# Identity products in TensorE's gaps, means in two column halves, a mask pattern made once, and a new order of work

## The chip, the cores and the metric

The kernel runs on one core of a Trainium2 chip. The metric is the device time of one execution in microseconds (us). A core has TensorE (PE, matrix products; loading of their stationary operand is shown as PEld), VectorE (DVE), ScalarE (ACT), GpSimd (POOL) and SyncE (SP, which issues all loads and stores here). Each engine works off its own list of instructions in order and waits on semaphores for the others.

## The reference

Sparse attention over 4 batches of 8 heads, 768 positions and 64 columns, followed by a two-branch layer:

```python
k_sum = k.reshape(B, H, nb, block, D).max(axis=3)      # block = 32, nb = 24
v_sum = v.reshape(B, H, nb, block, D).mean(axis=3)
scores_l = scale * q @ k.T      # kept where |i - j| < 16, else -1e9
scores_s = scale * q @ k_sum.T + log(32)
a = softmax(concat(scores_l, scores_s))
x = (a @ concat(v, v_sum))      # then heads side by side: 3072 x 512
out = maximum(x @ w1, x @ w2) @ w_out      # 512 -> 1024 -> 512
```

So each query sees at most 31 neighbours and all 24 block summaries.

## The kernel before

A helper records every operation as a task with its engine or engines, an estimated time, its inputs and outputs and a priority (`op`, line 107; `copy`, line 278, whose instructions all carry line 271 of `move`). Then `Plan.run` (line 132) walks through the tasks with these estimates, gives each engine the ready task of lowest priority number and buffers from rings, and so writes out one fixed order for each engine. The constants `C` (line 23) are priorities, the order of the loads (`first` for batch 0, `later` for the others) and which engines may do which copy. `caps` limits how many of the eight PSUM banks each kind of result may hold. On the chip nothing of the plan is left but the order and the semaphores.

Attention is done by batch and by pair of heads (`hp`, 0 to 3):

- `load_kq` (329) and `load_v` (337) load 384 KB of k or q of a pair, or 768 KB of v of four heads.
- `prep` (382): k and q are cast to bf16 (`kqb`), turned by six transposes each (line 393), and placed as `kx` and `qx`. For each of 12 tiles of 64 queries, `kx` holds 96 local keys and 24 block maxima (line 406), so that one product gives all 120 scores of a query.
- `place_v` (343): v is cast into `vx`, shifted copies are made for the odd tiles, and the block means are made by six products of 128 rows with `amean`, 256 columns wide (line 361), copied into `vx` and spread to all tiles.
- `scores` (425): 12 or 14 products for six tiles, each on 64 rows of the array (line 442). Two heads use the two halves of its rows. For batch 0 the mask is added by TensorE, with an identity times the pattern `hide` (434); for the others `pb` is multiplied by `mask` after the exponential (449, 454).
- `values` (462): 12 products on 64 columns of the array each (471), a reciprocal and a multiplication give x (482, 484); x of two pairs is turned by six transposes (494) and copied to `xt`.

The layer is rewritten: max(xw1, xw2) = xw1 + relu(x(w2 - w1)). `make_w12` (518) makes `wd` = w2 - w1 in four quarters and turns w1 (531); `make_w1o` (546) makes w1 @ w_out once (552, 32 products). `maxout` (560) then has, for each half batch of 384 rows (`grp`), 8 blocks of hidden columns of 4 products (567) with a relu each (572 on ACT, 574 on DVE), and three output tiles of 4 products with `w1o` (584) and 8 with `wo` (591), copied to `o` and stored.

TensorE has three ways of working here: the whole array, half its rows (scores) and half its columns (values). The planner counts 0.08 us (`TURN`) for a change between them, and when it has the choice it prefers a task in the mode that it is in:

```python
if e == "PE" and mode:
    able.sort(key=lambda t: t.mode != mode)
t = next((t for t in able if self.slots(t, now)), None)
```

`fixed_parts` (287) makes the constants: `hide` by wide memsets and selects on POOL (305 to 310), `amean` (313) and `mask` (323), also on POOL.

Of the kernel before, what the change touches and what calls it, by code (L numbers as in the profile page):

```python
# [15 lines left out]
BF16 = mybir.dt.bfloat16  # L16
# [7 lines left out]
    first='k2 v0 k0 k1 q1 q0 v1 b0 q2 b2 k3 q3 a0 a1 a2 b3 o3 b1 o0 a3 o1 o2',  # L24
    later='q0 q2 q3 k0 k1 v1 q1 k3 k2 v0',
    b0=dict(v=18, vcast=('POOL ACT', 'POOL'), vevac=('ACT DVE', 'DVE'), pair=22,
             scores=(40, 278), values=(-134, 64), kcast='DVE POOL ACT',
             qcast=('DVE', 'ACT POOL', 'DVE ACT', 'POOL DVE'), kplace='DVE',
             qplace=('ACT', 'ACT', 'ACT DVE', 'ACT DVE'),
             halo=('DVE POOL', 'DVE ACT', 'DVE ACT POOL', 'DVE POOL'), sums='DVE POOL',  # L30
             mask='PE', xt='ACT DVE'),
    b=dict(v=-590, vcast='ACT DVE', vevac='ACT DVE', pair=55, scores=(-12, 29),
             values=(-53, 1), kcast=('DVE POOL', 'DVE POOL', 'DVE ACT', 'DVE POOL'),
             qcast=('POOL DVE', 'ACT POOL', 'POOL', 'POOL DVE'),
             kplace=('ACT', 'DVE', 'DVE ACT', 'ACT'), qplace=('ACT', 'ACT', 'ACT', 'ACT DVE'),
             halo=('ACT', 'ACT', 'DVE', 'DVE POOL'),
             sums=('POOL', 'DVE POOL ACT', 'POOL', 'POOL'), mask='DVE POOL', xt='DVE'),
    w12=1950, w1t=-910, wo=430, w1o=-920, moe=1180, wd=('POOL', 'POOL', 'POOL', 'DVE POOL'),
    w1b=('POOL ACT', 'POOL DVE', 'POOL DVE', 'POOL ACT'),
    wocast=('POOL ACT DVE', 'POOL DVE', 'POOL', 'POOL'),  # L40
    w1tcopy=('ACT', 'ACT', 'ACT', 'ACT DVE'), w1ocopy='DVE', relu='ACT DVE', outcopy='ACT',
    caps=dict(kq=2, sc=7, av=8, mm=5, x=7))
# [52 lines left out]
class Plan:  # L95
# [11 lines left out]
    def op(self, engine, us, fn, read=(), write=(), change=(), touch=(), behind=(), prio=0.0, label="",  # L107
           mode="", port=False, dma=0.0):
# [3 lines left out]
        t.fn, t.label, t.mode, t.port, t.dma = fn, label, mode, port, dma  # L112
# [19 lines left out]
    def run(self):  # L132
# [20 lines left out]
        while len(order) < len(self.tasks):  # L153
            now = heapq.heappop(events)
            for e, queue in waiting.items():
# [3 lines left out]
                if e == "PE" and mode:  # L159
                    able.sort(key=lambda t: t.mode != mode)  # L160
# [32 lines left out]
def kernel(  # L193
# [48 lines left out]
    kxr = Ring(tiles("kx", 4, [128, NT, 128], BF16))  # L242
    qxr = Ring(tiles("qx", 4, [128, S], BF16))
# [23 lines left out]
    amean = const.tile([128, NM, 128], BF16, name="amean")  # L267
    hide_in, mask_in, amean_in = Buf(), Buf(), Buf()
# [18 lines left out]
    def fixed_parts():  # L287
# [16 lines left out]
        def make_hide():  # L304
            nc.gpsimd.memset(hide[:], 0.0)
            keep(hide[0:96], window - 1 - 16, 1, [[0, 2 * GN], [-1, 64]])
            keep(hide[0:96], window - 1 + 16, -1, [[0, 2 * GN], [1, 64]])
            keep(hide[96:128], nb - 1, -1, [[0, 2 * GN], [0, 64]])
            nc.gpsimd.memset(hide[0:64, 1, GN - 1, 48:64], NEG)
            nc.gpsimd.memset(hide[64:96, 1, GN - 1, 0:48], NEG)  # L310

        def make_amean():
            nc.gpsimd.memset(amean[:], 0.0)
            am = amean[:, :, 96:96 + nb]
# [6 lines left out]
        op("POOL", 4.0, make_hide, write=[hide_in], prio=-1, label="hide")  # L321
        op("POOL", 2.0, make_amean, write=[amean_in], prio=0.2, label="amean")
        op("POOL", 0.9, lambda: nc.gpsimd.tensor_scalar(
            out=mask[:], in0=hide[:], scalar1=-1.0 / NEG, scalar2=1.0, op0=ALU.mult, op1=ALU.add),
           read=[hide_in], write=[mask_in], prio=100, label="mask")
# [3 lines left out]
    def load_kq(b, hp, n, prio):  # L329
        f = kqin[b, hp, n] = Buf(kqf)  # L330
        op("SP", 1.06, lambda: nc.sync.dma_start(
            out=f.ap[:], in_=(k, q)[n][b, 2 * hp:2 * hp + 2].rearrange("h (p j) d -> p h (j d)", j=J)),
           write=[f], prio=prio, label=f"load {'kq'[n]}{b}{hp}", dma=0.52)
# [10 lines left out]
    def place_v(b, prio, cast_on, evac_on):  # L344

        lo, hi, means_at = slice(0, 64), slice(64, 128), slice(96, 128)
        for n in range(2):
# [6 lines left out]
            copy(on(cast_on, n, {"POOL": 1.52, "DVE": 0.98, "ACT": 1.42}), lambda f=f, h=h: (  # L354
# [4 lines left out]
            def means(ps=ps, h=h):  # L359
                for m in range(NM):  # L360
                    nc.tensor.matmul(out=bank(ps, 4 * D), lhsT=amean[:, m, :], rhs=vx[b].ap[:, 2 * m, h, 0:D],  # L361
                                     start=(m == 0), stop=(m == NM - 1))

            op("PE", 0.66, means, read=[even, amean_in], write=[ps], prio=prio + n, label=f"means {tag}")
            for i, (to, of, us) in enumerate((
                    ((lo, slice(1, NT, 2)), (hi, slice(0, NT, 2)), 0.55),
                    ((slice(64, 96), slice(1, NT - 1, 2)), (slice(0, 32), slice(2, NT, 2)), 0.45),
# [3 lines left out]
            copy(on(evac_on, n, {"DVE": 0.43, "ACT": 0.4}), lambda ps=ps, h=h: (  # L371
                vx[b].ap[means_at, 0, h, 0:D], bank(ps, 4 * D)[means_at].rearrange("p (h d) -> p h d", d=D)),
                 read=[ps, odd], write=[vx[b], means_in], prio=prio + n, label=f"means {tag}")
            copy({"DVE": 0.9}, lambda rows=rows: (
# [86 lines left out]
    def values(b, hp, grp, pb, prio, c):  # L461
# [17 lines left out]
        if hp == 0:  # L479
# [7 lines left out]
           read=[ps, inv], write=[x], prio=prio, label=f"x {tag}")  # L487
        if hp % 2 == 0:
            return
        xp = Buf(banks, "x")  # L490

        def turn():
            for n in range(2 * GU):
# [180 lines left out]
```

## Time and profile before

| | |
|---|---|
| median of 3 runs | 181.52 us (181.05 to 183.82) |
| the profiled execution | 182.66 us, its span 179.9 us |
| TensorE busy, instructions | 163.1 us, 1760 products |
| DVE, ACT, POOL busy | 108.1, 105.0, 64.2 us |
| read and written | 25.17 MB, 6.29 MB |
| mean granted TensorE clock | 0.997 |

How to read it: the span goes from the first to the last instruction of the profiled execution. Busy time says how long an engine had something in work; the lines of the 40 slices show when. The chain that ended last goes back from the last instruction, at each step to what released it, and in it each piece counts only for the time that it adds. A group in the timeline lasts until its last result is out, so it is longer there than in the chain, where the next group already runs beside its end. "[1.39 <-DVE kqb L271]" is an engine's idle time ahead of a group and what ended it.

### The profile page before, as it was taken

To read this page: it belongs to the slowest core of one execution; us is meant where nothing else is said; L and a number is where in the kernel's file an instruction comes from. 1 tells how busy PE (TensorE), PEld (TensorE's weight loads), DVE (VectorE), ACT (ScalarE), POOL (GpSimd) and SP (SyncE) were. 2 spreads that over 40 slices of the span, in tenths; PEclk is the share of its full clock that TensorE was granted. 3 is DMA by queue.
4 is the path that set the end of the run, shared out by engine and by line. 5 is a ranking of instruction groups with operands and counts; after the bars stand their busy time and mean duration, and the time that the engine had idled before them with its cause. 6 is when DMAs were issued, how large, how long until landed. Compare 5 with 4: busy or idle time off the path is not lost.

```text
span 179.9 us, 4266 instructions
## 1 busy us (share of the span) xinstructions
PE 163.1 (91%) x1760; PEld 95.9 (53%) x1760; DVE 108.1 (60%) x201; ACT 105.0 (58%) x167; POOL 64.2 (36%) x78
## 2 busy tenths in 40 slices
PE   0177995899999999999999999999999999999991
PEld 0154564666546554576545655666456545545540
DVE  0589699859989979899986662788854004000000
ACT  3546689697937528479786622688466345426421
POOL 8735469843505603045938330056430000000000
PEclk9999999999999999999999999999999999999998
DMA  5999999999999999998811101200111022012022
GB/s 148 281 303 328 388 390 391 396 231 308 304 308 250 285 300 231 272 319 251 284 73 58 62 0 61 96 24 4 58 62 60 0 114 65 0 58 112 4 105 70
DMA packets 42259, 31.72 MB, mean 176 GB/s; under 512 B 25856, under 2 KB 38144, under 8 KB 42240
## 3 DMA queue, kind: packets, MB, share of 16 engines
q1 hardware_dynamic: 42240, 31.46, 59.7%
q8 instruction: 13, 0.21, 0.5%
q14 instruction: 6, 0.05, 0.1%
HBM read 25.17 MB, written 6.29 MB: 175 GB/s over the span
## 4 chain that ended last, share of the span: by engine, by line
PE 85%; DVE 7%; DMA 4%; ACT 2%; issue 1%; SPq 0%; ACTq 0%; DVEq 0%
PE banks L591 24%; PE banks L567 23%; PE banks L584 12%; PE banks L393 6%; PE banks L471 4%; PE banks L442 4%; PE banks L552 4%; PE banks L361 4%; DMA vf<-in_v_dram 4%; PE banks L494 3%; DVE w1b L271 2%; DVE kx L271 2%; PE banks L434 1%; ACT vx L271 1%; DVE xs L484 1%; PE banks L531 1%
## 5 line engine op out<-in xcount | busy, mean ns | idle before, releaser
L567 PE MATMUL banks<-xt,wd 128*128 128x384 bf16 x256 | 47.3, 326 | 0.3 <-DVE xt L271 0.3
L591 PE MATMUL banks<-wo,g 128*128 128x512 bf16 x192 | 46.6, 380 | 0.0
L449 ACT ACTIVATE pb<-banks,bias 128x768 bf16<-128x768 f32 x32 | 27.6, 900 | 10.4 <-PE banks L442 9.7
L567 PEld LDWEIGHTS <-wd 128*128 128x128 bf16 x256 | 23.8, 98 | 15.0 <-issue 0.7
L572 ACT ACTIVATE g<-banks 128x384 bf16<-128x384 f32 x48 | 23.5, 492 | 13.3 <-PE banks L567 12.7
L271 POOL CAST kqb<-kqf 128x768 bf16<-128x768 f32 x19 | 17.8, 945 | 35.0 <-PE banks L393 13.4
L271 ACT COPY o<-banks 128x512 f32<-128x512 f32 x24 | 14.1, 586 | 27.1 <-PE banks L591 27.1
L591 PEld LDWEIGHTS <-g 128*128 128x128 bf16 x192 | 17.4, 98 | 18.2
L271 DVE COPY vx<-vx 64x1584 bf16<-64x1584 bf16 (+3 forms) x32 | 21.6, 687 | 4.4 <-ACT vx L271 3.7
L584 PE MATMUL banks<-w1o,xt 128*128 128x512 bf16 x96 | 23.2, 379 | 0.0
L393 PE MATMUL banks<-identity,kqb 128*128 128x128 bf16 x192 | 16.5, 234 | 6.6 <-ACT kqb L271 5.2
L454 POOL TENSOR_TENSOR pb<-pb,mask 128x768 bf16<-128x768 bf16 x9 | 15.0, 1675 | 14.2 <-ACT pb L449 14.2
L393 PEld LDWEIGHTS <-kqb 128*128 128x128 bf16 x192 | 13.4, 105 | 9.6 <-ACT kqb L271 5.2
L454 DVE TENSOR_TENSOR pb<-pb,mask 128x768 bf16<-128x768 bf16 x15 | 10.2, 687 | 11.3 <-ACT pb L449 11.2
L484 DVE TENSOR_TENSOR xs<-banks,inv 128x384 bf16<-128x384 f32 x32 | 16.5, 543 | 0.2
L271 ACT COPY qx<-banks 128x768 bf16<-128x768 bf16 x16 | 12.7, 803 | 5.3 <-PE banks L393 5.1
L406 DVE TENSOR_REDUCE ks<-kx 128x24 bf16<-128x768 bf16 x16 | 15.1, 945 | 0.1
L584 PEld LDWEIGHTS <-xt 128*128 128x128 bf16 x96 | 9.2, 98 | 10.1
L482 DVE RECIPROCAL inv<-banks 128x6 f32<-128x6 f32 x32 | 5.8, 190 | 11.2 <-PE banks L471 10.4
L442 PEld LDWEIGHTS <-kx 64*128 64x128 bf16 x416 | 7.8, 98 | 8.1 <-issue 5.0
L271 DVE COPY kx<-banks 128x768 bf16<-128x768 bf16 x9 | 8.6, 950 | 5.9 <-PE banks L393 5.8
L442 PE MATMUL banks<-qx,kx 64*128 64x64 bf16 (+2 forms) x416 | 9.9, 194 | 1.1 <-DVE kx L271 0.8
(56 smaller groups left out, 166.4 us busy)
## 6 DMA issues: line engine op xcount, KB each, us to landing
kqf<-in_k_dram SPq DMA_DIRECT2D x16, 384.0 KB, 6.0
vf<-in_v_dram SPq DMA_DIRECT2D x8, 768.0 KB, 8.6
kqf<-in_q_dram SPq DMA_DIRECT2D x16, 384.0 KB, 5.9
out_dram<-o SPq DMA_DIRECT2D x20, 256.0 KB, 2.0
wf<-in_moe_w_dram SPq DMA_DIRECT2D x8, 512.0 KB, 9.4
wf<-in_moe_w_out_dram SPq DMA_DIRECT2D x4, 512.0 KB, 9.3
out_dram<-o SPq DMA_DIRECT2D x4, 224.0 KB, 2.4
out_dram<-o SPq DMA_DIRECT2D x4, 32.0 KB, 2.9
```

The costliest lines, as they stand in the source:

```text
L271: {"DVE": nc.vector.tensor_copy, "ACT": nc.scalar.copy, "POOL": nc.gpsimd.tensor_copy}[engine](out=o, in_=i)
L361: nc.tensor.matmul(out=bank(ps, 4 * D), lhsT=amean[:, m, :], rhs=vx[b].ap[:, 2 * m, h, 0:D], start=(m == 0), stop=(m == NM - 1))
L393: nc.tensor.transpose(out=bank(ps, S, BF16)[:, 128 * j:128 * j + 128], in_=src.ap[:, j].rearrange("p h d -> p (h d)"), identity=identity[:])
L406: op("DVE", 0.95, lambda: nc.vector.tensor_reduce(out=ks.ap[:].rearrange("p (t s) -> p t s", s=2), in_=kx[b, hp].ap[:, :, 0:64].rearrange( ...
L442: nc.tensor.matmul(out=view()[:, a, 64 * i + n0:64 * i + n1], lhsT=kx[b, hp].ap[r, t], rhs=qx[b, hp].ap[r, at:at + n1 - n0], start=(c["mas ...
L449: op("ACT", 0.91, lambda: nc.scalar.activation(out=pb.ap[:].rearrange("p a t q -> p a (t q)"), in_=view(), func=ACT.Exp, bias=bias[:], sca ...
L454: nc.gpsimd if e == "POOL" else nc.vector).tensor_tensor(
L484: op("DVE", 0.55, lambda: nc.vector.tensor_tensor(out=x.ap[:, hp % 2], in0=av()[:, :, :, 0:D], in1=inv.ap[:].to_broadcast([128, GU, 2, D]) ...
L567: nc.tensor.matmul(out=bank(ps, GT), lhsT=wd[n // 2].ap[:, c, 128 * (n % 2):128 * (n % 2) + 128], rhs=x.ap[:, c, :], start=(c == 0), stop= ...
L572: nc.scalar.activation(out=g.ap[:, n, :], in_=bank(ps, GT), func=ACT.Relu)
L584: nc.tensor.matmul(out=bank(ps), lhsT=x.ap[:, c, sl], rhs=w1o[c].ap[:], start=(c == 0), stop=False)
L591: nc.tensor.matmul(out=bank(ps), lhsT=g.ap[:, f, sl], rhs=wo[f // 2].ap[:, f % 2, :], start=False, stop=(f == FC - 1))
```

## The change

1. Forty tasks of four products of the identity with itself (`warm`) may be given to TensorE wherever the planner finds nothing else able to run. They write a PSUM bank that nobody reads.
2. The means use an `amean` of 64 columns instead of 128 and make two column halves, two heads each: 12 products of 128 columns instead of 6 of 256, two copies out of PSUM instead of one, in the values' mode (`cols`).
3. The mask pattern of 64 columns is made once on POOL, repeated to 768 by DVE; `mask` is made on DVE too.
4. When TensorE is in the whole-array mode, a scores, values or means task that is alone of its mode stands behind other able tasks for up to 2 us of the plan (`hold`).
5. Each output tile of `w1o` is summed in four tasks of two products instead of two of four, so that each needs one quarter of the weights.
6. Order of loads, priorities, engine choices, `caps` and the planner's time estimates are new; all relus are on ACT. So the order of every engine is new, and some of the w1o products and of batch 1's transposes come ahead of the first hidden product.

Branches for `kqdma` and `xdma` (transposes by DMA) are added too, but both lists are empty; they are left out below, as are most of the estimates.

```diff
 C = dict(
-    first='k2 v0 k0 k1 q1 q0 v1 b0 q2 b2 k3 q3 a0 a1 a2 b3 o3 b1 o0 a3 o1 o2',
-    later='q0 q2 q3 k0 k1 v1 q1 k3 k2 v0',
...
-    w12=1950, w1t=-910, wo=430, w1o=-920, moe=1180, wd=('POOL', 'POOL', 'POOL', 'DVE POOL'),
...
-    w1tcopy=('ACT', 'ACT', 'ACT', 'ACT DVE'), w1ocopy='DVE', relu='ACT DVE', outcopy='ACT',
-    caps=dict(kq=2, sc=7, av=8, mm=5, x=7))
+    first='k2 v0 k1 k0 q1 q0 b0 k3 q3 a0 v1 b2 b3 q2 a1 o0 a3 a2 o1 o2 b1 o3',
+    later='q2 q0 k1 k3 k2 q3 q1 k0 v0 v1',
...
+    w12=2240, w1t=-1070, wo=1060, w1o=-830, moe=1300, wd='POOL',
...
+    relu='ACT', outcopy='ACT', caps=dict(kq=5, sc=6, av=6, mm=7, x=3, warm=1), hold=2, warm=40,
+    xdma=(), kqdma=(), tdma=1.5, hide=5.5, amean=8.5)
...
-                if e == "PE" and mode:
-                    able.sort(key=lambda t: t.mode != mode)
+                if e == "PE":
+                    many = {m: sum(t.mode == m for t in able) > 1 for m in ("rows", "cols")}
+                    able.sort(key=lambda t: t.fill or (t.mode != mode if mode else (
+                        t.mode != "" and not many[t.mode] and now < t.at + C["hold"])))
...
-    amean = const.tile([128, NM, 128], BF16, name="amean")
+    amean = const.tile([128, NM, 64], BF16, name="amean")
+    hide1 = const.tile([128, 64], BF16, name="hide1")
...
-            nc.gpsimd.memset(hide[:], 0.0)
-            keep(hide[0:96], window - 1 - 16, 1, [[0, 2 * GN], [-1, 64]])
-            keep(hide[0:96], window - 1 + 16, -1, [[0, 2 * GN], [1, 64]])
-            keep(hide[96:128], nb - 1, -1, [[0, 2 * GN], [0, 64]])
-            nc.gpsimd.memset(hide[0:64, 1, GN - 1, 48:64], NEG)
-            nc.gpsimd.memset(hide[64:96, 1, GN - 1, 0:48], NEG)
+            nc.gpsimd.memset(hide1[:], 0.0)
+            keep(hide1[0:96], window - 1 - 16, 1, [[-1, 64]])
+            keep(hide1[0:96], window - 1 + 16, -1, [[1, 64]])
+            keep(hide1[96:128], nb - 1, -1, [[0, 64]])
...
+        def spread_hide():
+            nc.vector.tensor_copy(out=hide[:].rearrange("p g t q -> p (g t) q"), in_=every_tile(hide1))
+            nc.vector.memset(hide[0:64, 1, GN - 1, 48:64], NEG)
+            nc.vector.memset(hide[64:96, 1, GN - 1, 0:48], NEG)
...
-        op("POOL", 0.9, lambda: nc.gpsimd.tensor_scalar(
+        op("DVE", 0.7, lambda: nc.vector.tensor_scalar(
...
-            def means(ps=ps, h=h):
+            def means(ps=ps, n=n):
                 for m in range(NM):
-                    nc.tensor.matmul(out=bank(ps, 4 * D), lhsT=amean[:, m, :], rhs=vx[b].ap[:, 2 * m, h, 0:D],
-                                     start=(m == 0), stop=(m == NM - 1))
-
-            op("PE", 0.66, means, read=[even, amean_in], write=[ps], prio=prio + n, label=f"means {tag}")
+                    for w in range(2):
+                        at = 4 * n + 2 * w
+                        nc.tensor.matmul(out=bank(ps, 2 * D)[64 * w:64 * w + 64], lhsT=amean[:, m],
+                                         rhs=vx[b].ap[:, 2 * m, at:at + 2, 0:D], start=(m == 0), stop=(m == NM - 1))
+
+            op("PE", 0.36, means, read=[even, amean_in], write=[ps], prio=prio + n, label=f"means {tag}",
+               mode="cols")
...
-            for n in range(2):
+            for n in range(4):
                 def mm(c=c, n=n, ps=ps):
-                    for f in range(4 * n, 4 * n + 4):
...
-                op("PE", 0.87, mm, read=[*w1t[2 * n:2 * n + 2], *wo[2 * n:2 * n + 2]], change=[ps],
-                   prio=prio, label=f"w1o {c}")
+                    for f in range(2 * n, 2 * n + 2):
+                        nc.tensor.matmul(out=bank(ps), lhsT=w1t[n].ap[:, f % 2, 128 * c:128 * c + 128],
+                                         rhs=wo[n].ap[:, f % 2, :], start=(f == 0), stop=(f == FC - 1))
+                op("PE", 0.44, mm, read=[w1t[n], wo[n]], change=[ps], prio=prio, label=f"w1o {c}")
...
+    for i in range(C["warm"]):
+        ps = Buf(banks, "warm")
+
+        def fill(ps=ps):
+            for n in range(4):
+                nc.tensor.matmul(out=bank(ps, 128), lhsT=identity[:], rhs=identity[:], start=True, stop=True)
+
+        op("PE", 0.23, fill, write=[ps], prio=1e6, label="warm", fill=True)
```

More of the change, by code (lines that the diff above doesn't have):

```diff
@@ new lines @@
+    b=dict(v=-315, vcast=('ACT DVE', 'ACT'), vevac='ACT', pair=95, scores=(43, 18),
+             values=(-92, -34), kcast=('DVE POOL ACT', 'POOL', 'DVE POOL', 'DVE POOL'),
+             qcast=('ACT POOL', 'DVE POOL ACT', 'DVE POOL ACT', 'POOL DVE'),
+             kplace=('ACT', 'ACT', 'DVE', 'DVE'), qplace=('ACT', 'DVE', 'ACT', 'ACT DVE'),
+             halo=('DVE ACT POOL', 'DVE ACT POOL', 'DVE ACT POOL', 'DVE ACT'),
+             sums=('POOL', 'DVE', 'DVE POOL', 'POOL'), mask='DVE POOL', xt='DVE'),
@@ L370, in place_v @@
                      write=[vx[b], odd, vh[b][n]], prio=prio + n, label=f"spread v{tag}{i}", port=True)
[L371 to L374, printed above, removed]
+            for w in range(2):
+                copy(on(evac_on, n, {"DVE": 0.3, "ACT": 0.3}), lambda ps=ps, n=n, w=w: (
+                    vx[b].ap[means_at, 0, 4 * n + 2 * w:4 * n + 2 * w + 2, 0:D],
+                    bank(ps, 2 * D)[64 * w + 32:64 * w + 64].rearrange("p (h d) -> p h d", d=D)),
+                     read=[ps, odd], write=[vx[b], means_in], prio=prio + n, label=f"means {tag}")
+            copy({"DVE": 1.06}, lambda rows=rows: (
                 rows(means_at, slice(1, NT)), rows(means_at, slice(0, 1)).to_broadcast([32, NT - 1, 4 * VW])),
```

93 lines of the change are left out of this document (57 added, 36 removed).

## The prediction

> **What bounds the kernel now.** I read the page first: busy shares, the 40 slices, the chain that ended last.
>
> ```profile
> span 179.9 us, 4266 instructions
> PE 163.1 (91%) x1760; PEld 95.9 (53%) x1760; DVE 108.1 (60%) x201; ACT 105.0 (58%) x167; POOL 64.2 (36%) x78
> ...
> PE   0177995899999999999999999999999999999991
> ...
> DMA  5999999999999999998811101200111022012022
> ...
> PE 85%; DVE 7%; DMA 4%; ACT 2%; issue 1%; SPq 0%; ACTq 0%; DVEq 0%
> ```
>
> TensorE is full from the eighth slice (about 32 us) to the end, and the chain is 85% TensorE. DMA is full in the first slices, while TensorE still has gaps. So there are two stages: a front, until the first product of the hidden layer (L567), and a TensorE-bound rest. Next the timeline of TensorE in the front, then of the casts that wait for loads.
>
> ```profile
> 5.23 0.82 PE L393 MATMUL banks<-identity,kqb 128*128 128x128 bf16 x6 [5.23 <-ACT kqb L271]
> 9.39 1.44 PE L361 MATMUL banks<-vx,amean 128*128 128x256 bf16 x6 [3.34 <-ACT vx L271]
> ...
> 14.15 0.82 PE L393 MATMUL banks<-identity,kqb 128*128 128x128 bf16 x6 [1.39 <-DVE kqb L271]
> ...
> 15.86 0.50 PE L442 MATMUL banks<-qx,kx 64*128 64x64 bf16 x12 [0.25 <-ACT qx L271]
> ...
> 22.99 0.51 PE L393 MATMUL banks<-identity,kqb 128*128 128x128 bf16 x6
> ...
> 33.90 0.32 PE L567 MATMUL banks<-xt,wd 128*128 128x384 bf16 x1 [0.32 <-DVE xt L271]
> ```
> ```profile
> 8.91 0.56 DVE L271 CAST kqb<-kqf 128x768 bf16<-128x768 f32 x1 [0.43 <-DMA kqf<-in_k_dram]
> ...
> 35.30 1.15 DVE L271 CAST kqb<-kqf 128x768 bf16<-128x768 f32 x1
> ```
> ```profile
> 20.43 2.07 POOL L271 CAST kqb<-kqf 128x768 bf16<-128x768 f32 x2 [3.27 <-DMA kqf<-in_k_dram]
> 24.01 2.36 POOL L521 TENSOR_TENSOR wd<-wf,wf 128x1024 bf16<-128x1024 f32 x1 [1.52 <-DMA wf<-in_moe_w_dram]
> ...
> 31.81 0.83 POOL L271 CAST kqb<-kqf 128x768 bf16<-128x768 f32 x1 [0.53 <-DMA kqf<-in_q_dram]
> ```
>
> The same six transposes last 0.82 us at 14.15 and 0.51 at 22.99 (an isolated end included), and six means 1.44 at 9.39 where the chain below has 0.66: TensorE runs at half rate until about 22 us, though the page's granted clock shows nothing of it. The hidden layer begins at 33.3 us (its first group follows an xt copy that ends there). In the chain the rest is gapless:
>
> ```profile
> 36.36 0.34 PE banks L393 x6
> 36.69 0.65 PE banks L567 x4
> ...
> 46.63 0.66 PE banks L361 x6
> 47.28 6.91 PE banks L552 x32
> ...
> 56.16 0.46 PE banks L442 x26
> 56.62 0.44 PE banks L393 x6
> 57.07 1.73 PE banks L584 x8
> ...
> 61.38 0.88 PE banks L471 x48
> 62.27 0.97 PE banks L591 x4
> ...
> 64.96 0.86 PE banks L591 x4
> ...
> 70.22 0.50 PE banks L471 x24
> ...
> 132.43 0.28 PE banks L442 x12
> ...
> 175.97 0.03 ACTq L271
> ```
>
> This gives prices at full rate: a transpose 0.34/6 = 0.056 us, a hidden product 0.65/4 = 0.163, a 512-column product 0.86/4 = 0.216. Scores: 26 cost 0.46 and 12 cost 0.28, so one is 0.013 and entering the mode 0.12. Values: 48 cost 0.88 and 24 cost 0.50, so one is 0.016, entering again 0.12. Leaving costs 0.11 (0.44 against 0.34, 0.97 against 0.86). I take 0.115 a switch.
>
> I counted matmuls and switches in the two built programs. Before, from the first hidden product on: 256 hidden x 0.163, 288 outputs and 32 of w1o x 0.216, 230 transposes x 0.056, 36 means x 0.109, 312 scores, 288 values, 53 switches: 142.1 us. Measured: 175.97 - 33.3 = 142.7. The sum holds within 0.6 us.
>
> **The change, part by part.** All of TensorE's order is new, so I redo the sum on the new order.
>
> The rest, from the first hidden product: 24 of the 32 w1o products now stand ahead of it (-5.2), as do 24 more transposes of k and q (-1.3), 6 of x and 8 of w1 (-0.8). Two calls of means stood ahead of it in both orders; the six behind it become 12 half-width products each. Two halves lie in different columns of the array; if they overlap as the values' halves do, a call is 6 x 0.056 = 0.33 instead of 0.66 (-1.9). But a call of means now enters and leaves a column mode: switches go from 53 to 64 (+1.3), in spite of the rule that groups wait for company. Sum: 142.1 - 5.2 - 1.3 - 0.8 - 1.9 + 1.3 = 134.1 us (terms unrounded). The means' ends are 0.33 and, with no overlap, 12 x 0.056 = 0.67, which costs 2.0 more. I take 0.33: the values are the nearest row, 12 of 65 columns in 0.19 us.
>
> The Trainium skill speaks against it: by "TensorEngine Tiling (Array Packing)", Restrictions and Gotchas, column tiling excludes the fast weight load, and "TensorE: Matmul & The Clock Gate", LDWEIGHTS, gives a load's columns divided by 1.2 ns, 53 ns for 64 columns. By that, 12 loads are an estimated 0.64 us, nothing is saved, and the sum is 1.9 us more. The values' groups load 64 columns for every product and still take 0.016 us each, so the trace disagrees and I go by it.
>
> When does the rest begin? In the new order four of batch 1's transposes stand ahead of the first hidden product; the last needs the load that stands 24th on SP's queue. Up to it there are 12 loads of k or q (384 KB), 2 of v (768) and 10 of weights (512): 11264 KB. The rate is in the windows:
>
> ```profile
> 25.00:30.00 5.00, 3.46 (x77) 2.33 (x76) 5.00 (x7) 4.84 (x7) 5.00 (x5) 1.00 1.08 395
> 30.00:35.00 5.00, 3.92 (x71) 2.99 (x72) 4.31 (x10) 3.17 (x4) 4.22 (x4) 1.00 1.06 396
> 40.00:60.00 20.00, 20.00 (x179) 11.64 (x178) 18.41 (x29) 14.81 (x22) 7.87 (x10) 1.00 1.09 291
> ```
>
> The load that landed at 31.81 was the last of 9088 KB; 2176 KB more at 396 GB/s is 5.6 us: 37.4 us. From the one at 20.43 (5248 KB) it would be 36.1 us. I take 37.4, the nearer row, and keep 36.1 for the range. Then a DVE cast (0.56 to 1.15, I take 0.7), the transposes (0.34) and 0.1 of handing over: the rest begins at 38.6 us, 5.3 later than now. The other inputs come earlier: the last q of batch 0 is the 14th load (6656 KB, about 25 us), its scores, exponentials and x follow within some 8 us, and ACT has three casts ahead of the xt copy, the last on a load of 9984 KB (34 us): xt by about 35.6.
>
> What hides the front's own work: ahead of 38.6 us TensorE has 21.7 us of useful work at full rate, 7 us more than before, and 160 small products (8.9 us). That fits in 37 us only if the clock is up early. The first 48 small products begin after the identity is made (1.08 + 0.29 us):
>
> ```profile
> 1.08 0.29 POOL masks.py:199 TENSOR_SCALAR_AFFINE_SELECT identity<-identity 128x128 bf16<-128x128 bf16 x1
> ...
> 2.13 2.84 POOL L301 TENSOR_SCALAR_AFFINE_SELECT hide<-hide 96x768 bf16<-96x768 bf16 x3
> ```
>
> They begin at 1.4 us and at the half rate of 0.137 us (0.82/6) end near 8 at the latest; k2's transposes, at 5.23 before, slip by up to 3 us. Nothing is queued that this delays to 38.6, and TensorE is then busy without a gap until the means of v0. I take the clock as full from there: cost nothing. If that cover is gone, see the last rival.
>
> The pattern: POOL's wide selects (2.84 us) become a twelfth as wide; DVE gains the repeat and the mask, two passes over 768 columns at about 0.56 each (the first cast's row) and two small fills, under 2 us ahead of 9 us. The first scores (15.86) wait for q, not for the pattern: nothing; price if exposed, those 2 us. Sixteen relus move from DVE to ACT:
>
> ```profile
> L572 ACT ACTIVATE g<-banks 128x384 bf16<-128x384 f32 x48 | 23.5, 492 | 13.3 <-PE banks L567 12.7
> L574 DVE TENSOR_SCALAR g<-banks 128x384 bf16<-128x384 f32 x16 | 8.7, 553 | 2.9 <-ACT g L572 2.1 <-PE banks L567 0.7
> ```
>
> That is 7.9 us more for ACT and 8.7 less for DVE, which was the fuller (18.41 of 20 us at 40 to 60). With the casts and placements that are dealt anew, the counts of the new program at the durations of before give ACT 116 us of work, 80 of it in the 110 us between first hidden product and last exponential. Cover enough: nothing. Stores are the same 28 and the tail after the last product the same 3.9 us (179.9 - 175.97).
>
> Behind the first hidden products wait wd's last quarter and wo's last. By bytes the former's load lands at 39.7, POOL's subtraction takes 2.36: 42.1, wanted at 38.6 + 4.2 = 42.8. The latter lands at 42.1, wanted cast at 44.1. Both fit with little to spare; I leave the 0.6 us by which the old sum missed as all the waiting there is, with 0 and 3 us as ends.
>
> Sum: 38.6 + 134.1 + 0.6 + 3.9 = 177.2 us of span, against 179.9: -2.7. The profiled execution took 182.66 us with what lies around its span, 1.1 above the median of 181.52. From the median: **178.8 us**.
>
> **Rivals.**
> 1. *The loads land as the earlier row says* (36.1): the rest begins at 37.3, 1.3 sooner, 177.5 us. For it: the same 390 GB/s. Against: wo's third quarter, cast by DVE, and 8 w1o products also stand ahead of the first hidden one.
> 2. *The half-width means save nothing*, by overlap or weight loads: +1.9, 180.7 us. Against: the row of the values.
> 3. *The two late quarters of weights stall TensorE* because SP's queue, in order, is held by a slot that is not free (the load of wd's last quarter needs POOL's cast of wo's first): each us late beyond 0.7 is a us; with 3 us late 181.1 us. Against: that cast can run from about 29 us on.
> 4. *TensorE stays at half rate in the front*, since the small products leave gaps: 21.7 us of work then takes up to twice as long, 43.4, the rest begins 4.8 later, 183.6 us, slower than before. It decides from a beginning at 41.3 us on. For it: before, the rate rose only at 22 us though TensorE worked from 14.15 on with one gap of 0.25. Against: 48 products in a row from 1.4 us.
>
> By the Trainium skill, "TensorE: Matmul & The Clock Gate", Part 1, the array starts at half rate and rises after a busy window of about 3.4 us; the rows agree with the half rate, and by the rule an estimated 8 us sees the rise, which speaks against rival 4.
>
> **How the numbers follow.** Forecast 0.47; rivals 1 to 4: 0.25, 0.11, 0.09, 0.08. The range of 176.0 to 182.6 us holds the forecast and rivals 1 to 3, with room below for rival 1 without the 0.6 of waiting and for runs as far below the median as the lowest shown (181.05), above for 2 and half of 3 together; 0.08 and some tails are left out. A difference of 2% (below 177.9, above 185.2) is about what a measurement of this kernel can tell from no change. Faster by that: most of rival 1 (0.20) and a little of the forecast (0.10): 0.30. Slower: a part of rival 4: 0.04. Within: 0.66.
>
> **What would show it.** Six transposes at 0.34 marginal (0.51 in the timeline) by 10 us, or rival 4. First hidden product at 38.6 with the cast of a k load just ahead of it; earlier is rival 1. Means groups of 0.33 plus a switch, against rival 2. TensorE without idle time after 39, or a wait on wd or wo between 42 and 46 (rival 3). I am wrong if the rest after the first hidden product is not 134 to 135 us long.

## The result, and the profile after

| | before | after |
|---|---|---|
| time, median (us) | 181.50 of 20 runs | 180.72 of 20 runs |
| lowest to highest | 180.85 to 183.82 | 179.59 to 183.38 |
| profiled execution: time, span | 182.66, 179.9 | 180.56, 178.9 |

The ratio is 0.9948, 95% interval 0.9923 to 0.9972: 0.5% faster, where 1.5% was forecast. Ratios, and the ranges of runs below, leave disturbed runs out (three of the 20 after). The sign and the stages came out as forecast, the size did not. Busy times, slices and granted clock of the page after:

```profile
span 178.9 us, 4689 instructions
PE 167.5 (94%) x1946; PEld 102.3 (57%) x1968; DVE 100.7 (56%) x193; ACT 115.0 (64%) x188; POOL 57.6 (32%) x74
PE   6999878999999999989999999999999999999991
PEclk9999999999999999999999999999999999999998
```

TensorE is busy from the first slice on now. Of its 167.5 us the small products are 13. TensorE in the front, from its timeline:

```profile
1.43 5.22 PE L666 MATMUL banks<-identity 128*128 128x128 bf16 x48 [1.43 <-POOL identity masks.py:199]
6.49 0.50 PE L422 MATMUL banks<-identity,kqb 128*128 128x128 bf16 x6
...
9.27 0.53 PE L379 MATMUL banks<-vx,amean 128*64 128x128 bf16 x12
...
25.74 0.51 PE L422 MATMUL banks<-identity,kqb 128*128 128x128 bf16 x6 [0.60 <-POOL kqb L277]
27.36 0.62 PE L573 MATMUL banks<-identity,w1b 128*128 128x128 bf16 x8 [1.11 <-POOL w1b L277]
...
33.22 1.89 PE L594 MATMUL banks<-wo,w1t 128*128 128x512 bf16 x7
```
```profile
37.60 0.56 DVE L277 CAST kqb<-kqf 128x768 bf16<-128x768 f32 x1 [0.90 <-DMA kqf<-in_k_dram]
```
```profile
38.68 0.81 PE L607 MATMUL banks<-xt,wd 128*128 128x384 bf16 x4
```

Six transposes last 0.50 us at 6.49 already (0.82 at 5.23 before), so TensorE is at full rate by then. The load that the forecast put at 37.4 has landed when its cast begins at 37.6, and the first hidden product begins at 38.7 (forecast 38.6). Twelve half-width means fit in 0.53 us with the isolated end included. What was not forecast stands behind that: rows of TensorE, ScalarE and VectorE between 50 and 79 us.

```profile
51.84 0.55 PE L478 MATMUL banks<-qx,kx 64*128 64x64 bf16 x26 [0.34 <-DVE qx L277]
...
75.51 1.48 ACT L277 CAST vx<-vf 128x1536 bf16<-128x1536 f32 x1 [1.00 <-DMA vf<-in_v_dram]
...
76.89 0.82 ACT L277 CAST kqb<-kqf 128x768 bf16<-128x768 f32 x1
77.02 0.57 DVE L277 COPY vx<-vx 64x1584 bf16<-64x1584 bf16 x1 [1.09 <-ACT vx L277]
...
77.61 1.17 DVE L277 CAST kqb<-kqf 128x768 bf16<-128x768 f32 x1
...
77.77 0.51 PE L422 MATMUL banks<-identity,kqb 128*128 128x128 bf16 x6 [0.29 <-ACT kqb L277]
...
78.84 0.51 PE L422 MATMUL banks<-identity,kqb 128*128 128x128 bf16 x6 [0.56 <-DVE kqb L277]
```

Read it from the bottom. TensorE waits for two casts of batch 2's k and q. ScalarE's (76.89) stands in its queue behind the cast of batch 3's v (75.51), and that one waited 1.00 us for its load. VectorE's (77.61) stands behind the first spread of the same v (77.02), which waited for ScalarE's cast. One late load so holds two queues in order, and through them TensorE, though the k and q of these casts had landed by 69.7 us. Measured from start to start of TensorE's products (the modelled end of a row hides part of a wait), the places cost 0.40 us at 51, 0.46 and 0.72 at 77 to 79, and 0.24 at 115.

The last products of TensorE after, and in the kernel f5 below, which has the same products and switches behind the first hidden one (38.76 us) but no wait:

```profile
171.72 3.19 PE L631 MATMUL banks<-wo,g 128*128 128x512 bf16 x13
```
```profile
171.80 1.46 PE L650 MATMUL banks<-wo,g 128*128 128x512 bf16 x6
```

The rest took 174.91 - 38.68 = 136.2 us after, and 173.26 - 38.76 = 134.5 us in f5. The forecast had 134.1 of work and 0.6 of waiting, 134.7.

### The profile page after: what moved, and what is told of

Read it like the earlier page. It is cut to its first block, busy times and chain, and to the rows that moved or that the text cites. A ratio compares the mean times of both kernels' runs of the same rounds, so it can differ in the third digit from the quotient of the medians.

```text
span 178.9 us, 4689 instructions
## 1 busy us (share of the span) xinstructions
PE 167.5 (94%) x1946; PEld 102.3 (57%) x1968; DVE 100.7 (56%) x193; ACT 115.0 (64%) x188; POOL 57.6 (32%) x74
## 4 chain that ended last, share of the span: by engine, by line
PE 70%; DMA 15%; issue 5%; DVE 4%; ACT 2%; SPq 1%; POOL 0%; POOLq 0%; DVEq 0%; ACTq 0%
PE banks L607 24%; PE banks L631 17%; PE banks L624 10%; DMA kqf<-in_q_dram 5%; DMA wf<-in_moe_w_out_dram 5%; DMA vf<-in_v_dram 4%; PE banks L478 3%; PE banks L507 3%; PE banks L422 3%; PE banks L594 3%; PE banks L666 3%; DVE kqb L277 2%; PE banks L536 2%; ACT vx L277 1%; PE banks L379 1%
## 5 line engine op out<-in xcount | busy, mean ns | idle before, releaser
L631 PE MATMUL banks<-wo,g 128*128 128x512 bf16 x181 | 44.7, 380 | 1.1 <-issue 0.8
L612 ACT ACTIVATE g<-banks 128x384 bf16<-128x384 f32 x64 | 31.3, 492 | 11.3 <-PE banks L607 10.8
L490 POOL TENSOR_TENSOR pb<-pb,mask 128x768 bf16<-128x768 bf16 x12 | 20.1, 1680 | 14.1 <-ACT pb L485 14.1
L277 DVE COPY vx<-vx 64x1584 bf16<-64x1584 bf16 (+3 forms) x32 | 19.8, 633 | 3.1 <-ACT vx L277 2.4
L277 POOL CAST kqb<-kqf 128x768 bf16<-128x768 f32 x11 | 10.5, 964 | 21.0 <-PE banks L422 12.7
L277 POOL COPY kx<-kx 128x32 bf16<-128x32 bf16 (+1 forms) x21 | 7.9, 409 | 26.5 <-ACT kx L277 25.1
L666 PE MATMUL banks<-identity 128*128 128x128 bf16 x160 | 13.0, 247 | 1.4 <-POOL identity masks.py:199 1.4
L277 DVE CAST kqb<-kqf 128x768 bf16<-128x768 f32 x10 | 7.7, 781 | 10.8 <-issue 7.1
L277 ACT CAST kqb<-kqf 128x768 bf16<-128x768 f32 x11 | 9.1, 832 | 5.7 <-DMA kqf<-in_k_dram 3.6
L666 PEld LDWEIGHTS <-identity 128*128 128x128 bf16 x160 | 11.6, 113 | 1.5 <-POOL identity masks.py:199 1.4
```

Of the source, the lines that this page charges most:

```text
L277: {"DVE": nc.vector.tensor_copy, "ACT": nc.scalar.copy, "POOL": nc.gpsimd.tensor_copy}[engine](out=o, in_=i)
L490: nc.gpsimd if e == "POOL" else nc.vector).tensor_tensor(
L612: nc.scalar.activation(out=g.ap[:, n, :], in_=bank(ps, GT), func=ACT.Relu)
L631: nc.tensor.matmul(out=bank(ps), lhsT=g.ap[:, f, sl], rhs=wo[f // 2].ap[:, f % 2, :], start=False, stop=(f == FC - 1))
L666: nc.tensor.matmul(out=bank(ps, 128), lhsT=identity[:], rhs=identity[:], start=True, stop=True)
```

## The experiments

All kernels but e2 are the kernel after with the edit shown. Edits of the order are made where the planner hands its list over, so that all else keeps its engine and place:

```diff
+        for move in C["moves"]:      # put a task behind another one in the list
+            shift(*move)
         for t in order:
-            t.fn(t.engine) if t.choice else t.fn()
+            if not t.fill:           # only in the kernels without small products
+                t.fn(t.engine) if t.choice else t.fn()
```

**The small products (e1, e2).** e1 leaves out all 160. e2 adds 144 to the kernel before:

```diff
+    small={'turn k02': 56, 'turn k00': 8, 'turn k01': 8, 'turn q01': 24},
+            if t.engine == "PE":
+                self.small(C["small"].get(t.label, 0))
         setup()
+        small(48)
```

> The kernel after with the 160 small products of the identity left out; every other instruction keeps its engine and its order. Theory (the front is set by loads and casts, the small products only fill TensorE's waiting): the first transposes run at the slow rate again, some 0.5 us of TensorE time is lost where it does not wait anyway, the first hidden product begins within 0.5 us of 38.8, and the time is 180.5 to 181.5 us. Rival (without them TensorE stays at half rate until about 22 us, as before, and that time is on the path): the first hidden product begins 2 to 5 us later and the time is 183 to 185 us.

e1: 181.28 us, ratio to before 0.9967 (0.9937 to 0.9997). The rival missed, and so did the theory on the front: the first hidden product began 1.7 us later (40.4). The time lies in the theory's range by luck, since the wait at 77 was not there: it was only 0.6 us longer (0.3 by the ratios). And its ten runs lay within 0.3 us of one another (181.11 to 181.39), where those of the kernel after reach from 179.6 to 182.0.

> The kernel before with 144 small products of the identity added (48 ahead of everything, 56 behind the first turn, 8, 8 and 24 behind the next ones), and nothing else changed. The run without them after the change had its first hidden product 1.7 us later than the kernel after, so they do take time out of the front there. Theory (the front is a chain of TensorE, casts and placings in turn, and TensorE's half-rate part lies on it): the first hidden product begins 1 to 2.5 us ahead of 33.1 us. Rival (in this order VectorE's placings and casts set the front whatever TensorE does): less than 0.5 us. The time follows, 179.0 to 180.5 us against 181.0 to 181.5.

e2: 182.99 us, ratio 1.0065 (1.0035 to 1.0095). The rival held for the front: the first hidden product stayed (33.3 us against 33.1). TensorE ran at full rate early and waited longer for the casts. The time lies above both ranges, with a new wait of 0.79 us for a cast of k at 38.

**The waits in the rest (e3, e7, e8, a2).** e3 puts the waiting casts ahead of the v cast and spread:

```diff
+    moves=(('cast v30', 'ACT', ('means 21', 'ACT')), ('spread v300', 'DVE', ('cast v30', 'ACT')),
+        ('spread v101', 'DVE', ('place q11', 'DVE')), ('spread v102', 'DVE', ('spread v101', 'DVE')),
+        ('turn k32', 'PE', ('hidden 201', 'PE'))),
```

> The kernel after with five of its instructions' groups put later in their queues and nothing else changed: batch 3's first cast of v behind ScalarE's cast of k20 and the copies of the means, its first spread behind VectorE's cast of q21, two spreads of batch 1's v behind the placing of q11, and one turn behind two hidden products. Theory (the waits of 0.40 us at 51.1, 0.46 at 77.3, 0.72 at 78.1 and 0.24 at 114.8 are the term that the forecast put too low, and they come from the order of the queues): they go, 1.2 to 1.8 us, and the time is 178.9 to 179.5 us. Rival (the work is only late next somewhere else, so that what one wait gives back another takes): a change of less than 0.4 us, 180.3 to 181.1 us.

e3: 181.42 us, ratio 0.9967 (0.9925 to 1.0009). The four waits were gone from the trace, but the spreads, now in one block on VectorE, made the placing of a q late and TensorE waited 0.82 us at 80.8. The first hidden product, too, began 0.7 us later (39.4). The rival held: the wait moved. e7 mends it at the source. It issues the load of batch 3's v first, keeps the other edits, and e8 is e7 without small products:

```diff
+    moves=(*[(x, 'SP', ('load v30', 'SP')) for x in
+             ('load q32', 'store 002', 'store 001', 'load k20', 'load q21')],
+        ('spread v101', 'DVE', ('place q11', 'DVE')), ('spread v102', 'DVE', ('spread v101', 'DVE')),
+        ('turn k32', 'PE', ('hidden 201', 'PE'))),
```

> The kernel after with one load of batch 3's v issued ahead of the two loads, two stores and one load that stand before it on SyncE's queue, the placing of q11 ahead of two spreads on VectorE, and one turn behind two hidden products; no engine's work changes. Theory (the lost 1.2 us at 77 to 79 us hang on when that load lands, and so does most of the kernel's spread from run to run): v lands about 3 us earlier, none of the four waits is left, the profiled span is 176.9 to 177.6 us, the time 178.6 to 179.5 us and the runs spread less. Rival (another load or store is late in its place): 180 us or more, with a new wait of 0.5 us or more between 60 and 90 us.

> The same three moves, and the 160 small products left out. If the small products bring 1.7 us in the front and the waits had taken it back, this is 1.3 to 1.9 us slower than the same kernel with them. If they bring only what the run without them showed in all (0.5 us), it is 0.3 to 0.7 us slower.

> The kernel after once more, as measure for the other runs on this chip: 180 to 181.3 us. Theory (the wait for batch 3's v at 77 us varies with the landing of the load): the sum of TensorE's waits behind the first hidden product differs from the 1.8 us of the first trace by about as much as the span differs from 178.9 us. Rival (the spread has its place in the front or in the clock): the waits are the same 1.8 us and the difference lies elsewhere.

e7: 181.43 us, ratio 0.9982 (0.9947 to 1.0016). e8: 180.57 us, ratio 0.9939 (0.9918 to 0.9959). a2: 182.02 us, ratio 0.9995 (0.9961 to 1.0028). In e7 and e8 no wait is left behind the first hidden product. Yet e7 was not faster, and leaving the small products out made it faster and steady (180.41 to 180.77), against both expectations of e8. In a2 the wait at 77 was absent from the trace and the span was longer all the same, 180.0 us: the first hidden product began at 41.0, with a wait of 0.60 us at 35 for a cast of the output weights. The spread had a place in the front after all, as a2's rival had it. The windows of a2 with TensorE's granted clock (third from the end; 0.59 is the mean of a stretch that lies mostly at 0.50, the half clock):

```profile
24.00:28.00 4.00, 2.14 (x40) 1.65 (x39) 3.07 (x6) 2.92 (x5) 2.05 (x3) 0.98 1.08 389
28.00:32.00 4.00, 3.95 (x63) 2.35 (x63) 1.17 (x4) 2.89 (x4) 3.15 (x2) 0.59 1.07 396
```

Of the 11 runs of a2 eight had a mean clock of 0.985 to 0.991 and spans of 179.9 to 180.9 us, three had 0.996 to 1.0 and 178.2 to 179.6.

**The loads (e4).**

```diff
+        cs = slice(0, KC if i == 0 or n == 1 else 1)
-            out=f.ap[:], in_=(moe_w1, moe_w2)[i].rearrange(...)[:, :, 256 * n:256 * n + 256]),
+            out=f.ap[:, cs], in_=(moe_w1, moe_w2)[i].rearrange(...)[:, cs, 256 * n:256 * n + 256]),
```

> The kernel after with three of the four loads of the second weight matrix cut to a quarter, and the subtraction that reads them reading that quarter four times over, so the difference of the weights is not the reference's. That takes 1.15 MB, about 2.9 us of the loads at 390 GB/s, out of the way of everything that is loaded behind them. Theory of the forecast (the 24th load sets the begin of the hidden products): the first hidden product begins 2 to 3 us earlier and the time is 177.7 to 178.7 us. Rival (TensorE is without a gap from 33.2 us on and ahead of that waits for casts in their queues, so that earlier loads give it nothing to do sooner): less than 0.6 us, 180.0 to 181.0 us.

e4: 179.71 us, ratio 0.9858 (0.9795 to 0.9922), four runs. Between the two: the first hidden product at 37.9, 0.8 us earlier for 2.9 us less of loads, and no wait at 77. The loads hold the front in part only.

**The cast of the output weights (f5, f6, g3).** e1 and e8 lost their 1.7 us in one place, a wait of TensorE at 33 us for VectorE's cast of the second quarter of the output weights. That cast in the kernel after, and in e1:

```profile
29.74 5.64 POOL L563 TENSOR_TENSOR wd<-wf,wf 128x1024 bf16<-128x1024 f32 x2 [1.29 <-DMA wf<-in_moe_w_dram]
32.26 0.90 DVE L277 CAST wo<-wf 128x1024 bf16<-128x1024 f32 x1
```
```profile
29.15 5.18 POOL L564 TENSOR_TENSOR wd<-wf,wf 128x1024 bf16<-128x1024 f32 x2
32.20 2.68 DVE L278 CAST wo<-wf 128x1024 bf16<-128x1024 f32 x1
```

The same cast lasts 0.90 or 2.68 us. GpSimd makes two subtractions in a row; in e1 they began 0.6 us earlier, so the cast found the second one running and ended 0.55 us after it. By the Trainium skill, "SBUF — State Buffer", "SBUF: two separate sides", VectorE and GpSimd share a pair of ports as an exclusive lock, which the instruction that starts first holds to its end; the two rows agree. f5 is e8 and f6 is e7, with that cast on ScalarE:

```diff
+        next(t for t in order if t.label == "wo 1").engine = "ACT"
```

> The kernel with v's load moved up and no small products, and the cast of the second quarter of the output weights moved from VectorE to ScalarE. There VectorE's cast lasted 2.70 us (0.90 us in the kernel after), beside GpSimd's two subtractions, and TensorE waited 1.7 us for it at 33.2 us. Theory (that one cast, early or late against GpSimd, decides 1.7 us of the front): ScalarE needs about 1.05 us from 32.2 us on, the first hidden product begins at 38.6 to 39.2 instead of 40.4, and the time falls from 180.6 to 178.8 to 179.4 us. Rival (the k and q loads that land at 37 to 38 us hold it as the forecast had it, or ScalarE's own queue is late in its place): 179.8 to 180.6 us.

> The same with the small products. Theory (they add nothing to the path once the cast is out of the way, but the clock that the throttle grants falls to 0.50 for some 3.5 us at 28 to 33 us in part of the executions): runs at full clock within 0.4 us of the kernel without them, the others 1 to 2 us above, the median 0.3 to 1.5 us above. Rival (the small products bring 1 us or more in the front): the fastest runs 1 us or more below those without them.

f5: 179.02 us, ratio 0.9851 (0.9820 to 0.9882), all runs within 0.2 us. f6: 180.47 us, ratio 0.9914 (0.9879 to 0.9949), from 179.25 to 181.31. f5's theory held, and f6's in the median: the small products bring nothing once the cast is out of the way, and cost 1.45 us. But of f6's five runs at full clock (0.997 or more) only two lie within 0.4 us of f5's median; the others are up to 1.4 us above it. f5's cast and first hidden product:

```profile
31.95 1.05 ACT L296 CAST wo<-wf 128x1024 bf16<-128x1024 f32 x1
...
38.76 0.81 PE L626 MATMUL banks<-xt,wd 128*128 128x384 bf16 x4
```

g3 has that cast's edit alone, without small products:

> The kernel after without its small products and with the cast of the second quarter of the output weights on ScalarE, the rest of its order as it was (v's load, the two spreads and the turn not moved). Theory (the wait for v at 77 us is there when TensorE comes early and the load lands late, and was hidden behind the 1.7 us that the cast cost in the run without small products): the waits of 0.4 us at 51 and 0.24 us at 115 are back, and of the 1.2 us at 77 to 79 us some or all, 179.6 to 180.9 us. Rival (the load lands early whenever there are no small products): 179.5 to 179.8 us with no wait between 76 and 79 us.

g3: 179.87 us, ratio 0.9878 (0.9830 to 0.9925). The wait at 51 us is back. Its profiled run (span 177.6) shows no wait of TensorE at 77, but its spans reach from 177.3 to 179.0 us where f5's stay within 177.2 to 177.4. So the three moves take the spread out; that it is v's load in the longer runs is argued, since no trace caught one.

**Which small products bring the half clock, and why (g1, g2, h1, h2, h3).** g1 and g2 are f5 with a part of them:

```diff
+            if not t.fill or n < first:      # g1: the 48 ahead of the first turn; g2: n > first
```

> The kernel of 179.0 us (v's load moved up, the cast of the output weights on ScalarE, no small products) with the first 48 small products back, those ahead of the first turn. Theory A (the drop of the granted clock to 0.50 is moved from about 24 us, where TensorE waits anyway, to 28 to 33 us by TensorE's early work at full rate, so that the early ones suffice for it only if they keep the rate up): with nothing behind them TensorE is at half rate again by 9.4 us, and the time is 178.8 to 179.4 us with little spread. Theory B (any products ahead of the first turn move it): 180 to 181 us in half of the executions.

> The kernel of 179.0 us with the other 112 small products back, those in the gaps from 6.8 to 21.9 us. Theory A (it is the filled gaps between 6 and 22 us that move the drop of the clock onto the path): the median is 0.6 to 1.6 us above 179.0 and the runs spread over 1.5 us or more, with a granted clock of 0.50 between 28 and 33 us in the slower ones. Theory B (the first 48 do it): 178.8 to 179.4 us with little spread.

g1: 178.77 us, ratio 0.9819 (0.9773 to 0.9864), within 0.4 us. g2: 180.80 us, ratio 0.9909 (0.9868 to 0.9949), from 179.03 to 181.67. It is those in the gaps that cost, as theory A of both had it. Windows of g1, of g2, and of f1 (no small products, below):

```profile
4.00:8.00 4.00, 2.29 (x32) 2.22 (x31) 0.89 (x2) 1.69 (x3) 1.08 (x4) 1.00 1.26 256
8.00:12.00 4.00, 2.29 (x24) 1.72 (x23) 3.00 (x8) 3.47 (x5) 0.00 (x0) 0.55 1.06 372
```
```profile
24.00:28.00 4.00, 2.28 (x44) 1.59 (x39) 3.11 (x6) 3.18 (x6) 1.97 (x3) 1.00 1.05 382
28.00:32.00 4.00, 4.00 (x63) 2.47 (x65) 1.01 (x4) 2.83 (x4) 3.66 (x2) 0.57 1.08 398
```
```profile
20.00:24.00 4.00, 2.01 (x47) 1.59 (x41) 3.55 (x9) 4.00 (x6) 0.63 (x2) 1.00 1.08 383
24.00:28.00 4.00, 4.00 (x52) 2.54 (x49) 1.63 (x5) 2.97 (x5) 2.23 (x3) 0.57 1.08 393
```

In all three the clock halves right behind a stretch in which TensorE was busy for only about half of 4 us. Not every such stretch does it: the kernel after's trace has 2.29 us at 24 to 28 too, and its clock stays at 1.00. Where no gap is filled, that stretch lies early, and the half clock falls where TensorE would wait again. Where the gaps up to 22 us are filled, the one left at 25 to 28 us stands just ahead of the dense work, and the half clock falls on that. If so, filling it must help:

```diff
+            if t.engine == "PE":
+                self.small({"turn x011": 10, "turn q02": 22}.get(t.label, 0))
```

> The kernel with v's load moved up, the cast of the output weights on ScalarE and all 160 small products, and 32 more of them in TensorE's two waits at 25 to 28 us (10 behind the turn of x011, 22 behind the turn of q02). Theory (the clock falls to 0.50 for 3.4 us because TensorE waits about 2 us out of 3.4 there, and whether it does in an execution hangs on where a window of the clock's control begins): with the waits filled it does not fall, the time is 178.9 to 179.6 us, and the runs lie within 0.7 us of one another. Rival (it falls for another reason, such as TensorE's long activity before): the same as without the 32, 180.0 to 180.9 us with 2 us of spread.

> The kernel after itself with the same 32 small products added and nothing moved. Theory: no granted clock of 0.50 before 36 us; the waits for the placing of q11 (0.4 us), for v (0 to 1.2 us), at 115 us (0.24 us) and the slow cast of the output weights stay: 179.6 to 180.8 us. Rival: 180.5 to 182 us as in the run again.

> The kernel of the first of these three without its 32 added products, once more, as measure on this chip: 179.3 to 181.3 us, the median 180.0 to 180.9, a granted clock of 0.988 to 0.991 in more than half of the executions.

h1 (f6 with that gap filled): 179.50 us, ratio 0.9875 (0.9829 to 0.9920), within 0.55 us. h2 (the kernel after with it): 180.80 us, ratio 0.9956 (0.9920 to 0.9992). h3: 179.70 us, ratio 0.9884 (0.9840 to 0.9928). h1's windows:

```profile
24.00:28.00 4.00, 4.00 (x81) 3.51 (x80) 3.42 (x6) 3.52 (x6) 2.15 (x2) 1.00 1.08 390
28.00:32.00 4.00, 3.84 (x77) 2.52 (x76) 1.99 (x6) 3.09 (x4) 3.32 (x3) 1.00 1.06 391
```

In all 18 runs of h1 and h2 the mean clock was 0.995 or more; in f6 and h3, with the gap open, it was 0.987 to 0.990 in 8 of 18. Seven of these are f6's, which ran on another chip. h3, on the chip of h1 and h2, had it in one of six runs, against its expectation, so neither this count nor the times of h1 and h3 settle the cause alone. The traces do more. In every one, each change of the granted clock lies a whole number of 3.41 us behind the first change, which falls elsewhere in each execution (in a2 at 7.36 us and then 6 and 7 times 3.41 us later). The stretches of that grid around the gap, in a2 and in the kernel after:

```profile
24.43:27.84 3.41, 1.55 (x28) 1.21 (x23) 2.67 (x4) 2.48 (x5) 1.91 (x2) 1.00 1.07 390
27.84:31.25 3.41, 3.41 (x51) 2.04 (x51) 0.69 (x1) 2.14 (x3) 2.53 (x2) 0.50 1.08 395
```
```profile
23.50:26.92 3.42, 2.14 (x38) 1.45 (x36) 2.99 (x6) 2.97 (x6) 1.62 (x2) 1.00 1.08 388
26.92:30.33 3.41, 2.92 (x64) 1.93 (x66) 0.84 (x3) 2.47 (x4) 2.01 (x3) 1.00 1.06 386
```

In a2 one stretch holds the whole gap, and the clock halves at its end; in the kernel after an edge at 26.92 us cuts the gap in two, and it does not. In the seven traces with such a fall before 30 us (a2, e7, f1, f6, g1, g2, h3) TensorE was busy for 1.3 to 1.7 us of the 3.41 us just before the fall. So the gap is the cause in these traces, and in each execution the place of the grid decides whether it counts. That the untraced runs follow this is argued. h2 was no faster than the kernel after, and its trace had a wait of 0.98 us at 52: at full clock the waits of the rest remain.

**The means and the company (f1, f2, e5).** f1 and e5 make the means as six products of full width, f2 sets the planner's `hold` to 0; f1 and f2 without small products, to be compared with e1.

```diff
-                    for w in range(2):
-                        nc.tensor.matmul(out=bank(ps, 2 * D)[64 * w:64 * w + 64], lhsT=amean[:, m],
-                                         rhs=vx[b].ap[:, 2 * m, at:at + 2, 0:D], ...)
+                    nc.tensor.matmul(out=bank(ps, 4 * D), lhsT=amean[:, m],
+                                     rhs=vx[b].ap[:, 2 * m, 4 * n:4 * n + 4, 0:D], ...)
```

> The kernel after without its small products, whose runs lay within 0.3 us of one another (181.3 us), and with the means as six products of the full width. Theory (0.33 us and two switches of about 0.115 us against 0.66 us): TensorE's work behind the first hidden product is 0.1 us a call longer, the time 181.5 to 182.1 us. Rival (the halves share nothing and the switches come on top): 180.4 to 181.0 us.

> The kernel after with each call's means as six products of the full width instead of twelve of half the width, in the same place of the order. Theory (0.33 us for the half-width call and 0.23 us for its two switches against 0.66): the rest of the path is longer by 5 or 6 calls times 0.1 us, and the time is 180.9 to 181.3 us. Rival (two products on two halves of the columns share nothing, so that twelve of them cost what six cost, and the switches come on top): the time is 179.0 to 180.0 us.

> The kernel after without its small products, with the planner's wait for company set from 2 us to 0. The plan has 100 switches of TensorE's mode instead of 83 and the order changes on every engine. Theory: 17 switches at 0.115 us are 2.0 us, 182.5 to 184 us. Rival (groups that wait cost as much in places as the switches they spare): 180.8 to 181.8 us.

f1: 182.87 us, ratio 1.0059 (1.0035 to 1.0083), 1.6 us above e1. e5: 183.64 us, ratio 1.0068 (1.0025 to 1.0112), but 181.5 to 182.3 us in the four runs with a clock of 1.0; in seven of the other eight it was 0.989 to 0.991. The means behind the first hidden product in the kernel after, and in f1:

```profile
L379 PE MATMUL banks<-vx,amean 128*64 128x128 bf16 x72 | 3.1, 221 | 0.0
```
```profile
L378 PE MATMUL banks<-vx,amean 128*128 128x256 bf16 x36 | 5.0, 274 | 0.0
```

That is 1.9 us for six calls, what the forecast had; the expectations of f1 and e5 were too low because they spared the full-width calls their switches, but their neighbours in the order work on half the columns, and 63 of 64 switches stay. f2: 183.04 us, ratio 1.0077 (1.0052 to 1.0101), 1.76 us above e1. From the start of the first hidden to that of the last product TensorE took 136.4 us against e1's 134.7, with 81 switches against 64: about 0.10 us a switch, if the switches are all of the difference. Waiting for company is worth its place.

## Why the prediction was wrong, point by point

- *TensorE at full rate early* (against rival 4): right, it was by 6.5 us.
- *The first hidden product at 38.6*: right in size (38.7), wrong in reason. With 2.9 us less of loads ahead it came only 0.8 us earlier (e4), and TensorE had no gap from 33.2 us on. One cast beside GpSimd decides 1.7 us there (e1, f5), and the half clock 1.1 to 1.6 (the first hidden product at 40.4 in h3's trace, 39.3 in h1's with the gap filled, 38.8 in f5's without small products). The sentence "I take the clock as full from there: cost nothing" does not hold in part of the runs.
- *TensorE's work behind it*: right, 134.5 us in f5 with no wait, for 134.1 and the 0.6 by which the old sum missed. Half-width means and switches cost what the rows of before gave; rival 2 fell (f1), and with it the estimate of 0.64 us for 12 loads that the forecast worked out from the Trainium skill: in the kernel after the next group begins 0.46 us behind the first of the 12 products (9.27 to 9.73), which is 0.33 and a switch.
- *Pattern, relus, late quarters of wd and wo* (rival 3): no wait of TensorE in the trace is for them. ScalarE was busy 115.0 us, for 116 forecast.
- *Waiting*: the step that failed, "I leave the 0.6 us by which the old sum missed as all the waiting there is". In the profiled run the waits add to 0.40 + 0.46 + 0.72 + 0.24 = 1.8 us, 1.2 of them at 77 to 79 us, and the rest took 136.2 us for 134.7. With 0.1 each in the front and the tail that is the span of 178.9 us for 177.2. What the old sum missed was no measure of it (in f5, without a wait, the new sum misses 0.4): the new order of loads puts v last, and no step looked at what stands behind v's cast in ScalarE's and VectorE's queues.
- In part of the runs the half clock comes on top, but in this measurement it is the smaller part: 14 of the 17 runs behind the ratio had a mean clock of 0.995 or more, and their median span is 178.4 us, 1.2 above the forecast's 177.2. With the other three (0.986 to 0.991, spans 179.6 to 180.0) the median is 178.6. What each untraced run waited for stays open, since a trace shows one run.

f5, with those costs taken out and no small products, has a span of 177.2 us, the sum of the forecast: 38.8 + 134.5 + 3.9.

The best versions, g1 (0.9819) and f5 (0.9851), beat both kernels: the new order and the half-width means, without the small products in the gaps, with v's load first and that cast on ScalarE.

## What to carry to other kernels

Prices from the rows of a dense stretch carry over to a new order of the same work; its waits do not, so walk each engine's queue and ask what stands behind every instruction that waits for a load. Filling TensorE's gaps gains nothing where casts or loads set the pace, and it matters which gap is left: one just ahead of the dense stretch can put a half clock on it. When runs spread, compare their granted clock and take several traces; one trace shows one outcome.

## What the runs showed of the hardware

- The granted clock changed only on a grid of 3.41 us, which began at another time in each execution. It halved behind a stretch of the grid in which TensorE was busy for 1.3 to 1.7 us, in gaps of 1.3 us and less in a2 (0.94 and 1.25 us, start to start less the product's price). In the fronts, stretches with 1.8 us or more never led to a fall, and one with 1.69 us (e5) did not either. In a2 the half clock lasted 3.4 us, by windows of single microseconds (0.92 in one, 0.50 in three, 0.88 in one). By the Trainium skill, "TensorE: Matmul & The Clock Gate", "Why this matters for your kernels", the advice for keeping the rate is no idle gap above about 3 us; here shorter ones, two in a row, were enough to lose it.
- In f5 TensorE ran at half rate until about 19 us (six transposes 0.82 us, hide products 0.82) under a granted clock of 1.00; in g1, after 48 small products and a gap of 3.2 us, the same stretch shows 0.50. A clock of 1.00 ahead of the first change says nothing of the rate.
